# Prologue of a sketched-attention and FFN kernel: key features and kv sums in 32-column tiles, a third of the key products on GpSimd, and another order of the first loads

## The chip, the cores and the metric

The kernel runs on one core of one Trainium2 chip. The metric is the device time of a run in microseconds; a kernel's time is the median of its runs. Engines are named as the profile names them: PE is TensorE's matmul (PEld its weight loads), DVE is VectorE, ACT is ScalarE, POOL is GpSimd, SP is SyncE, which here only issues transfers. A name like "q1" below is a piece of a tensor and is explained where it is used first.

## The reference

The inputs are q, k and v of shape (4 batches, 4 heads, 1088 positions, 32), the two sketches S1 and S2 (8 x 32 each), w_in (128 x 2048) and w_out (2048 x 128), all float32.

```python
def phi(x):                                   # 64 features of a position
    a = einsum('rd,bhsd->bhsr', S1, x)
    b = einsum('rd,bhsd->bhsr', S2, x)
    return einsum('bhsi,bhsj->bhsij', a, b).reshape(..., 64)
q_p, k_p = phi(q), phi(k)
kv = einsum('bhsf,bhsd->bhfd', k_p, v)        # 64 x 32 per head
z = sum(k_p, axis=2)
num = einsum('bhsf,bhfd->bhsd', q_p, kv)
den = einsum('bhsf,bhf->bhs', q_p, z) + 1e-6
x = (num / den) as (4352 tokens, 128)
out = maximum(x @ w_in, 0) ** 2 @ w_out       # (4352, 128)
```

## The kernel before

The attention part is small; the FFN part, 4352 tokens through 128 x 2048 and 2048 x 128, keeps TensorE busy from about 14 us to the end. Tokens are columns of one tile, xT (128 x 4352), and the FFN goes over them in ten chunks (the list FC: 256, 384, 448, 448, 512 ... 256 columns). For every chunk 16 blocks of 128 hidden units are made: `pg` (L582, w_in times xT), a relu on ScalarE (L591), a square on ScalarE or VectorE (L599, L601), and `po` (L620, w_out times the square, summed over the blocks). Chunk 0 is columns 0 to 255 of batch 0, chunk 1 is columns 256 to 639.

Attention of batch 0 is split into three pieces of 256, 384 and 448 columns. The first piece is done by a prologue written out by hand (L678 to L810), so that the FFN can start before the rest. Everything behind it is put in order by a small planner at build time (`_Order`): each task has an engine, an estimated duration and a key, and the planner emits the instructions of all engines in the order of its simulated schedule. The engines then run their own queues strictly in that order; the planner does not see what the chip does.

The prologue, in the order that matters:

- Loads. S1 and S2 are issued by ScalarE (L216, L217), then two of the four first v parts; all else is issued by SyncE: k in two parts (columns 0 to 511 and 512 to 1087), q's first 256 columns (q0), v (four parts for tiles 0 to 3, then four for tiles 4 to 8), q's columns 256 to 639 (q1), w_in in four quarters (wi0 to wi3, 256 KB each), q's columns 640 on (q2), w_out in four quarters (wo0 to wo3, 256 KB each). There are eight landing semaphores used in turn by all loads, so an issue waits in its queue until the load eight places before it has landed.
- `keep_warm` (L668) makes ten matmuls of constants while the loads run.
- k is transposed by VectorE (`a_kT0`, L287) into kt0; S1 and S2, side by side in s_nat, into s_T (L681). Small copies on three engines spread s_T into the block forms sf (L686, for k) and sq (L689 to L696, for q).
- `a_kf` (L310): one matmul per tile of 128 positions, kt0 as weights (128 x 128), sf as the moving side (64 columns); it gives both sketches of k in PSUM (kf). ScalarE copies the second half to kb (L319). A float32 matmul appears in the trace as two passes, so that nine matmuls are 18 records.
- `a_kp0` (L326): VectorE multiplies kf by kb to the 64 features of each head, in four instructions of 2, 2, 3 and 2 tiles.
- `q0(x)` (L719) makes both sketches of q's first 256 columns (x0); ScalarE copies one (qb0), VectorE multiplies (qp0, L741).
- `a_kv0` (L380): per tile and head one matmul with 64 columns of features as weights and 32 columns of v and 32 of ones as the moving side, summed in PSUM (kvp).
- From kvp VectorE makes block-diagonal weights bd (L757), a copy kvt (L766) and zm (L768). TensorE makes den and num of the first piece (L783) and two helper products (L790, L426); VectorE divides (L803 to L808) and writes xT's columns 0 to 255.

GpSimd, besides small copies, casts w_in's quarters into the type that the `pg` matmuls take (`cast_wi`, L663). Its queue then holds the 16 copies `rd` (`a_rl`, L491) that bring the reciprocals of the second piece of batch 0 (columns 256 to 639) into place; they come after the fourth cast, in program order and by an explicit dependence on ("wi", 3). VectorE turns rd into bc (L545) and multiplies it with nd to xT (L552), which chunk 1 of the FFN reads.

## Time and profile before

| What | Value |
|---|---|
| median of 3 runs | 187.94 us (187.44 to 187.97) |
| span of the profiled execution | 185.6 us |
| rest of a run, median less span | 2.3 us |
| first FFN product (L582) starts | 13.73 us |
| FFN chunk 1 (128x384 `pg`) starts | 21.99 us |
| PE busy | 180.1 us, 97% of the span |
| DVE, ACT, POOL busy | 59%, 79%, 19% |
| HBM read and written | 8.78 MB and 2.23 MB |

The profile is of one execution. Times are counted from the start of its span, in us; the profile has no separate total time for that execution, so that the 2.3 us around the span are the median of the runs less this span. In a line of groups or of the time line, "out<-in" are the program's names, then come the shape, a count, and in brackets the idle time of the engine before the group with what ended it. "Landing" of a transfer is the moment at which all its parts are reported as written.

### The profile page before, as it was taken

Reading aid. Unit: us, or ns where it says so; the run is one execution under the profiler, and the core shown is the slowest. Engines: PE = TensorE matmul, PEld = TensorE weight load, DVE = VectorE, ACT = ScalarE, POOL = GpSimd, SP = SyncE. Lnnn points to the kernel's source line nnn. Section 1 sums busy time; section 2 is a strip of 40 time slices with the busy share of each in tenths; the row PEclk is TensorE's granted clock in tenths of the full one; section 3 lists DMA queues with packets and bytes.
Section 4 is the critical chain, followed back from the end, with each engine's and each line's share of the span. In section 5 each row is a group of like instructions: output and inputs, shape, how many; then the busy total and the mean of one; then the engine's idle time right before and its main releaser. Section 6 shows DMA issues by size and latency. Waiting matters only on the chain.

```text
span 185.6 us, 3865 instructions
## 1 busy us (share of the span) xinstructions
PE 180.1 (97%) x1466; PEld 104.9 (57%) x1466; DVE 109.4 (59%) x244; ACT 147.4 (79%) x282; POOL 35.5 (19%) x157
## 2 busy tenths in 40 slices
PE   8898999999999999999999999999999999999992
PEld 2766766666656556554454545554555555555791
DVE  4979889958991699599343982996121113112210
ACT  3509778878978989699797996897999999988960
POOL 2725405327400000770000003820000000000000
PEclk9999999999999999999999999999999999999999
DMA  5799900100039600000882100001203000300111
GB/s 176 188 285 322 203 8 5 28 4 0 4 43 250 159 4 0 4 0 8 189 218 42 16 0 4 0 0 22 38 0 58 0 0 5 56 0 0 28 28 28
DMA packets 24673, 11.25 MB, mean 61 GB/s; under 512 B 18000, under 2 KB 23120, under 8 KB 24656
## 3 DMA queue, kind: packets, MB, share of 16 engines
q1 hardware_dynamic: 24144, 10.82, 24.8%
q10 hardware_dynamic: 512, 0.20, 0.4%
q8 instruction: 11, 0.18, 0.4%
q14 instruction: 6, 0.05, 0.1%
HBM read 8.78 MB, written 2.23 MB: 59 GB/s over the span
## 4 chain that ended last, share of the span: by engine, by line
PE 95%; DMA 1%; DVE 1%; ACT 0%; issue 0%; POOL 0%; ACTq 0%; DVEq 0%
PE po L620 60%; PE pg L582 18%; PE nd L535 3%; PE kvp L401 2%; PE pol L615 2%; PE po L615 2%; PE qc L303 2%; DMA s_nat<-in_S_dram 1%; PE kvp L383 1%; PE kf L313 1%; PE kc L303 1%; PE x L722 1%; ACT gt L591 0%; PE warm L671 0%; PE num L783 0%; PE den L783 0%
## 5 line engine op out<-in xcount | busy, mean ns | idle before, releaser
L620 PE MATMUL po<-g,w_o 128*128 128x512 f32 (+3 forms) x288 | 133.2, 546 | 0.0
L582 PE MATMUL pg<-xT,w_in 128*128 128x512 f32 (+3 forms) x160 | 104.5, 663 | 0.5 <-ACT gt L591 0.5
L591 ACT ACTIVATE gt<-pg 128x512 f32<-128x512 f32 (+3 forms) x145 | 80.9, 562 | 21.2 <-PE pg L582 20.5
L599 ACT ACTIVATE g<-gt 128x512 f32<-128x512 f32 (+2 forms) x123 | 72.0, 602 | 2.6
L620 PEld LDWEIGHTS po<-g,w_o 128*128 128x128 f32 x288 | 53.0, 189 | 29.8 <-issue 19.9
L582 PEld LDWEIGHTS pg<-xT,w_in 128*128 128x128 f32 x160 | 30.0, 189 | 31.7 <-issue 15.0
L601 DVE TENSOR_TENSOR g<-gt 128x512 f32<-128x512 f32 (+2 forms) x22 | 14.2, 651 | 41.8 <-ACT gt L591 41.8
L442 POOL COPY kv<-kvt 32x64 f32<-32x64 f32 x48 | 11.6, 241 | 64.7 <-DVE kvt L419 62.6
L496 POOL COPY rd<-rc 32x9 f32<-32x9 f32 (+2 forms) x80 | 16.6, 207 | 12.5 <-DVE rc L488 9.3
L505 DVE STREAM_SHUFFLE qa<-qc 128x576 f32<-128x576 f32 (+2 forms) x20 | 11.6, 647 | 0.0
L520 DVE TENSOR_TENSOR qp<-qa,qb 128x576 f32<-128x576 f32 (+2 forms) x20 | 10.8, 599 | 0.0
L624 DVE STREAM_TRANSPOSE oT<-po 128x512 f32<-128x512 f32 (+3 forms) x9 | 5.9, 652 | 8.1 <-PE po L620 8.1
L468 DVE STREAM_TRANSPOSE qt<-qc 128x576 f32<-128x576 f32 (+2 forms) x10 | 5.8, 614 | 6.0 <-PE qc L303 6.0
L354 DVE TENSOR_TENSOR kp<-fs 128x576 f32<-128x576 f32 x12 | 8.2, 741 | 0.0
L535 PE MATMUL nd<-qp,kv 32*32 32x288 f32 (+2 forms) x320 | 6.8, 353 | 0.0
L552 DVE TENSOR_TENSOR xT<-nd,bc 128x576 fp32r<-128x576 f32 (+2 forms) x10 | 5.6, 600 | 1.1 <-PE nd L535 1.1
L545 DVE STREAM_TRANSPOSE bc<-rd 128x576 f32<-128x576 f32 (+2 forms) x10 | 5.8, 598 | 0.7 <-POOL rd L496 0.6
L345 DVE STREAM_TRANSPOSE fs<-kc 128x576 f32<-128x576 f32 x6 | 4.3, 762 | 3.1 <-PE kc L303 3.1
L535 PEld LDWEIGHTS nd<-qp,kv 32*32 32x32 f32 x320 | 3.8, 103 | 4.0 <-issue 2.2
L505 DVE STREAM_SHUFFLE qb<-qc 128x576 f32<-128x576 f32 (+2 forms) x10 | 6.0, 648 | 0.0
L296 DVE STREAM_TRANSPOSE qT<-qn 128x192 f32<-128x192 f32 (+3 forms) x11 | 5.8, 562 | 0.0
L615 PE MATMUL pol<-w_o,g 128*128 128x128 f32 x32 | 5.7, 275 | 0.0
(94 smaller groups left out, 94.2 us busy)
## 6 DMA issues: line engine op xcount, KB each, us to landing
kn<-in_k_dram SPq DMA_DIRECT2D x3, 544.0 KB, 5.3
qn<-in_q_dram SPq DMA_DIRECT2D x3, 544.0 KB, 6.6
vn<-in_v_dram SPq DMA_DIRECT2D x9, 144.0 KB, 5.2
w_in<-in_moe_w_in_dram SPq DMA_DIRECT2D x4, 256.0 KB, 5.0
w_o<-in_moe_w_out_dram SPq DMA_DIRECT2D x4, 256.0 KB, 7.7
out_dram<-oT SPq DMA_DIRECT2D x12, 64.0 KB, 2.0
out_dram<-oT SPq DMA_DIRECT2D x8, 56.0 KB, 1.9
out_dram<-oT SPq DMA_DIRECT2D x8, 48.0 KB, 1.8
```

Of the source, the lines that this page charges most:

```text
L354: nc.vector.tensor_tensor(out=_ap(st[b, "kp"], 0, 128, 2 * o, [[64, NT], [8, 8], [1, 8]]), in0=_ap(fs, 0, 128, o, [[32, NT], [1, 8], [0, 8]]),
L442: nc.gpsimd.tensor_copy(_ap(st[b, "kv"], 32 * c, 32, 64 * h, [[32, E], [1, 32]]), _ap(st["kvt"], 32 * h, 32, 0, [[64, E], [1, 32]]),)
L496: nc.gpsimd.tensor_copy(st[b, "rd", i0][32 * h : 32 * h + 32, n * c : n * c + n], st["rc"][32 * c : 32 * c + 32, n * h : n * h + n],)
L505: nc.vector.stream_shuffle(in_=banks(st[b, "qc", i0], 2 * x, 0, m), out=_ap(st[b, which, i0], 0, 128, 2 * m * x, [[m, 2], [1, m]]), mask=m ...
L520: nc.vector.tensor_tensor(out=st[b, "qp", i0, e][:, r], in0=st[b, f"qa{e}", i0][:, r], in1=st[b, "qb", i0][:, r], op=mult,)
L535: nc.tensor.matmul(nd[32 * h : 32 * h + 32, 512 * c : 512 * c + m], kv[r, o : o + 32], qp[r, m * h : m * h + m], start=(e == 0), stop=(e = ...
L582: nc.tensor.matmul(st["pg", u][:, n * i : n * i + n], w_in[:, 128 * (d0 + i) : 128 * (d0 + i) + 128], xT[:, c0 : c0 + n],)
L591: nc.scalar.activation(gt[:, 0:w], st["pg", u][:, 0:w], Relu)
L599: nc.scalar.activation(g2[:, 0:w], gt[:, 0:w], Square)
L601: nc.vector.tensor_tensor(out=g2[:, 0:w], in0=gt[:, 0:w], in1=gt[:, 0:w], op=mult)
L615: nc.tensor.matmul(po[x // 128][:, 0:128], g[:, x : x + 128], w, start=(d == 0), stop=(d == NB - 1),)
L620: nc.tensor.matmul(po[0][:, 0:n], w, g, start=(d == 0), stop=(d == NB - 1))
```

## The change

- S2 is issued first on ScalarE's queue; S1 goes second on SyncE's, behind the first part of k. The second part of k and q0 go to ScalarE's queue, all eight v parts to SyncE's.
- The weights and the rest of q come in the order wi0, q1, wo0, wi1, wo1, wi2, wo2, q2, wi3, wo3 (before: q1, wi0, wi1, q2, wo0, wi2, wi3, wo1, wo2, wo3).
- Nine constant matmuls in place of ten.
- On GpSimd the four irep copies and two memsets come before the copies that wait for s_T, and the two sw copies behind them; it takes over one sf copy and two sq copies. VectorE's sf copies go to ScalarE (two) and GpSimd.
- VectorE transposes s_T before k, and k in the order tiles 0 to 3, 7 to 8, 4 to 6.
- `a_kf` makes four matmuls of 32 columns per tile in place of one of 128; `a_kv0` makes two of 32 in place of one of 64.
- Tiles are grouped as 2, 2, 2 and 3. The product of the last three (128x768) is made by GpSimd; for it ScalarE copies both halves of kf (192 columns, kab) out of PSUM.
- On VectorE, qT of columns 256 to 447 and s2f stand ahead of bd, the other qT (448 to 639) behind it; kvt is copied by ScalarE.
- The instruction in L776, a GpSimd copy that only made its queue wait for kp, is gone.

The planner and all behind the prologue are unchanged, and so is the order of instructions there on each engine.

```diff
-    W0, W3, W4 = 10, 1, 1
+    POOL_T = 6
+    W0, W3, W4 = 9, 1, 1
...
-    nc.scalar.dma_start(s_nat[0:8, :], S1[:, :])
+    load_k(nc.sync, 0, 0, 512)
     nc.scalar.dma_start(s_nat[8:16, :], S2[:, :])
-    load_k(nc.sync, 0, 0, 512)
-    load_k(nc.sync, 0, 512, S)
-    load_q(nc.sync, 0, 0, 256)
+    nc.sync.dma_start(s_nat[0:8, :], S1[:, :])
+    load_k(nc.scalar, 0, 512, S)
+    load_q(nc.scalar, 0, 0, 256)
...
-    load_v(nc.sync, 0, 0, 0, 4)
-    load_v(nc.scalar, 0, 2, 0, 4)
-    load_v(nc.sync, 0, 1, 0, 4)
-    load_v(nc.scalar, 0, 3, 0, 4)
+    for p in range(4):
+        load_v(nc.sync, 0, p, 0, 4)
     for p in range(4):
         load_v(nc.sync, 0, p, 4, NT)
+    load_wi(nc.sync, 0)
     load_q(nc.sync, 0, 256, 640)
-    load_wi(nc.sync, 0)
+    load_wo(nc.sync, 0)
     load_wi(nc.sync, 1)
+    load_wo(nc.sync, 1)
+    load_wi(nc.sync, 2)
+    load_wo(nc.sync, 2)
     load_q(nc.sync, 0, 640, S)
-    load_wo(nc.sync, 0)
-    load_wi(nc.sync, 2)
     load_wi(nc.sync, 3)
-    load_wo(nc.sync, 1)
-    load_wo(nc.sync, 2)
     load_wo(nc.sync, 3)
...
-    def a_kf(t0, n, pool, tag):
+    def a_kf(t0, n, pool, tag, pool_too=False):
         kf = pool.tile([128, 512], F32, tag=tag, name="kf")
         for t in range(n):
-            nc.tensor.matmul(
-                _ap(kf, 0, 128, 32 * t, [[32 * n, 2], [1, 32]]),
-                kt0[:, 128 * (t0 + t) : 128 * (t0 + t) + 128],
-                sf[:, 0:64],
-            )
-        kb = wpool.tile([128, 32 * 3], F32, tag="kb", bufs=4, name="kb")
-        nc.scalar.copy(kb[:, 0 : 32 * n], kf[:, 32 * n : 64 * n])
+            for c in range(4):
+                o = 128 * (t0 + t) + 32 * c
+                nc.tensor.matmul(
+                    _ap(kf, 32 * c, 32, 32 * t, [[32 * n, 2], [1, 32]]),
+                    kt0[:, o : o + 32],
+                    sf[:, 0:64],
+                )
+        if pool_too:
+            kb = wpool.tile([128, 64 * 3], F32, tag="kab", bufs=1, name="kab")
+            nc.scalar.copy(kb[:, 0 : 64 * n], kf[:, 0 : 64 * n])
+        else:
+            kb = wpool.tile([128, 32 * 2], F32, tag="kb", bufs=3, name="kb")
+            nc.scalar.copy(kb[:, 0 : 32 * n], kf[:, 32 * n : 64 * n])
...
-        nc.vector.tensor_tensor(
+        own = t0 == POOL_T
+        (nc.gpsimd if own else nc.vector).tensor_tensor(
...
     def a_kv0(t):
         for h in range(H):
-            i, y, o, o_v = h % 2, h // 2, 64 * (H * t + h), 32 * (NT * h + t)
-            nc.tensor.matmul(
-                st[0, "kvp"][64 * i : 64 * i + 64, 64 * y : 64 * y + 64],
-                st[0, "kp"][:, o : o + 64],
...
+            i, y, o_v = h % 2, h // 2, 32 * (NT * h + t)
+            for x in range(2):
+                r, o = 64 * i + 32 * x, 64 * (H * t + h) + 32 * x
+                nc.tensor.matmul(
+                    st[0, "kvp"][r : r + 32, 64 * y : 64 * y + 64],
+                    st[0, "kp"][:, o : o + 32],
...
-    a_kf(2, 2, psf, "pg")
-    a_kf(4, 3, psf, "po")
-    a_kf(7, 2, psf, "pg")
+    a_kf(2, 2, psf, "po")
+    a_kf(6, 3, psf, "pg", True)
+    a_kf(4, 2, psf, "pg")
...
-    for t0, n in ((0, 2), (2, 2), (4, 3), (7, 2)):
+    for t0, n in ((0, 2), (2, 2), (4, 2), (6, 3)):
...
-    nc.vector.transpose(s2f[:, :], _ap(sf, 0, 128, 72, [[0, 4], [1, 8]]))
...
-    for i0 in (8, 14):
-        a_qT(0, i0, 6)
+    a_qT(0, 8, 6)
+    nc.vector.transpose(s2f[:, :], _ap(sf, 0, 128, 72, [[0, 4], [1, 8]]))
...
-    nc.vector.tensor_copy(st["kvt"][:, :], st[0, "kvp"][:, 0:128])
+    nc.scalar.copy(st["kvt"][:, :], st[0, "kvp"][:, 0:128])
...
     a_bd(0)
+    a_qT(0, 14, 6)
...
-    nc.gpsimd.tensor_copy(zero_a[:, 0:1], st[0, "kp"][:, 256 * NT - 1 : 256 * NT])
```

More of the change, by code (lines that the diff above doesn't have):

```diff
@@ L261 @@
     make_identity(nc, iden[:])
+    for h in range(H):
+        nc.gpsimd.tensor_copy(
+            _ap(irep, 32 * h, 32, 0, [[32, 4], [1, 32]]),
+            _ap(iden, 32 * h, 32, 32 * h, [[0, 4], [1, 32]]),
+        )
+    nc.gpsimd.memset(_ap(vn[1], 96, 32, 32 * (NT - 2), [[32 * NT, H], [1, 64]]), 0.0)
+    nc.gpsimd.memset(_ap(pd, 0, 128, 8, [[9, 4 * NT], [1, 1]]), 1e-6)
     own_f, s2f, zm = sb("own_f", 16), sb("s2f", 32), sb("zm", 32)
@@ L307, in sketch @@
                 )
-    def a_kf(t0, n, pool, tag):
+    def a_kf(t0, n, pool, tag, pool_too=False):
         kf = pool.tile([128, 512], F32, tag=tag, name="kf")
         for t in range(n):
-            nc.tensor.matmul(
-                _ap(kf, 0, 128, 32 * t, [[32 * n, 2], [1, 32]]),
-                kt0[:, 128 * (t0 + t) : 128 * (t0 + t) + 128],
-                sf[:, 0:64],
-            )
-        kb = wpool.tile([128, 32 * 3], F32, tag="kb", bufs=4, name="kb")
-        nc.scalar.copy(kb[:, 0 : 32 * n], kf[:, 32 * n : 64 * n])
+            for c in range(4):
[4 more added lines that the diff above has]
+                    sf[:, 0:64],
+                )
+        if pool_too:
[4 more added lines that the diff above has]
+            nc.scalar.copy(kb[:, 0 : 32 * n], kf[:, 32 * n : 64 * n])
         st["kf", t0] = kf, kb
@@ L328, in a_kp0 @@
         kf, kb = st["kf", t0]
-        nc.vector.tensor_tensor(
+        own = t0 == POOL_T
+        (nc.gpsimd if own else nc.vector).tensor_tensor(
             out=_ap(st[0, "kp"], 0, 128, 256 * t0, [[64, 4 * n], [8, 8], [1, 8]]),
-            in0=_ap(kf, 0, 128, 0, [[8, 4 * n], [1, 8], [0, 8]]),
-            in1=_ap(kb, 0, 128, 0, [[8, 4 * n], [0, 8], [1, 8]]),
+            in0=_ap(kb if own else kf, 0, 128, 0, [[8, 4 * n], [1, 8], [0, 8]]),
+            in1=_ap(kb, 0, 128, 32 * n if own else 0, [[8, 4 * n], [0, 8], [1, 8]]),
             op=mult,
@@ L381, in a_kv0 @@
         for h in range(H):
-            i, y, o, o_v = h % 2, h // 2, 64 * (H * t + h), 32 * (NT * h + t)
-            nc.tensor.matmul(
-                st[0, "kvp"][64 * i : 64 * i + 64, 64 * y : 64 * y + 64],
-                st[0, "kp"][:, o : o + 64],
-                _ap(vn[0], 0, 128, o_v, [[VC - o_v, 2], [1, 32]]),
-                start=(t == 0 and y == 0),
-                stop=(t == NT - 1),
-                skip_group_check=True,
-            )
+            i, y, o_v = h % 2, h // 2, 32 * (NT * h + t)
[4 more added lines that the diff above has]
+                    st[0, "kp"][:, o : o + 32],
+                    _ap(vn[0], 0, 128, o_v, [[VC - o_v, 2], [1, 32]]),
+                    start=(t == 0 and y == 0),
+                    stop=(t == NT - 1),
+                    skip_group_check=True,
+                )
     def a_kv(b, t, x, start=False):
@@ L679 @@
     keep_warm(W0)
+    nc.vector.transpose(s_T[:, :], s_nat[:, :])
     a_kT0(0, 4)
-    nc.vector.transpose(s_T[:, :], s_nat[:, :])
+    a_kT0(7, 2)
+    a_kT0(4, 3)
     for h, eng in (
-        (0, nc.gpsimd.tensor_copy), (1, nc.vector.tensor_copy), (2, nc.scalar.copy),
-        (3, nc.vector.tensor_copy),
+        (0, nc.gpsimd.tensor_copy), (1, nc.scalar.copy), (2, nc.gpsimd.tensor_copy),
+        (3, nc.scalar.copy),
     ):
@@ L694 @@
     )
-    for h, eng in ((1, nc.scalar.copy), (2, nc.gpsimd.tensor_copy), (3, nc.scalar.copy)):
-        eng(
+    for h in range(1, H):
+        nc.gpsimd.tensor_copy(
             _ap(sq, 32 * h, 32, 64 * (h % 2), [[128, 2], [1, 64]]),
@@ L701 @@
         nc.gpsimd.tensor_copy(sf[32 * h : 32 * h + 32, 64:96], s_T[:, :])
-    for h in range(H):
-        nc.gpsimd.tensor_copy(
-            _ap(irep, 32 * h, 32, 0, [[32, 4], [1, 32]]),
-            _ap(iden, 32 * h, 32, 32 * h, [[0, 4], [1, 32]]),
-        )
-    nc.gpsimd.memset(_ap(vn[1], 96, 32, 32 * (NT - 2), [[32 * NT, H], [1, 64]]), 0.0)
-    for w in sw:
-        nc.gpsimd.tensor_copy(w[:, :], sf[:, 64:96])
-    nc.gpsimd.memset(_ap(pd, 0, 128, 8, [[9, 4 * NT], [1, 1]]), 1e-6)
-    a_kT0(4, 3)
-    a_kT0(7, 2)
     a_qT(0, 0, 8)
@@ L733 @@
     nc.scalar.copy(_ap(qb0, 0, 128, 0, [[256, 2], [1, 256]]), banks(x0, 0, 0, 256))
-    st[0, "kvp"] = psf.tile([128, 512], F32, tag="pg", name="kvp")
-    for t0, n in ((0, 2), (2, 2), (4, 3), (7, 2)):
+    st[0, "kvp"] = psf.tile([128, 512], F32, tag="po", name="kvp")
+    for t0, n in ((0, 2), (2, 2), (4, 2), (6, 3)):
         a_kp0(t0, n)
@@ L738 @@
             a_kv0(t)
-    nc.vector.transpose(s2f[:, :], _ap(sf, 0, 128, 72, [[0, 4], [1, 8]]))
+    for w in sw:
+        nc.gpsimd.tensor_copy(w[:, :], sf[:, 64:96])
     nc.vector.tensor_tensor(
```

## The prediction

> **What bounds the kernel now.** I read the page's first part, then the chain that ended last in order of time, then the time line from 13 to 22 us, then the transfers one by one, with times to landing.

> ```profile
> PE 180.1 (97%) x1466; PEld 104.9 (57%) x1466; DVE 109.4 (59%) x244; ACT 147.4 (79%) x282; POOL 35.5 (19%) x157
> ...
> PEclk9999999999999999999999999999999999999999
> ```

> TensorE is busy for 97% of the span at full clock. Only the start, where PE waits or does small work, can give anything back.

> ```profile
> 1.54 2.73 DMA s_nat<-in_S_dram
> ...
> 5.18 2.19 PE kf L313 x18
> 7.37 1.06 PE x L722 x8
> 8.44 2.25 PE kvp L383 x72
> 10.69 0.58 PE den L747 x4
> ```

> The chain (start, duration) begins with the landing of S1 and S2 at 4.27. Then come k features, x0, the kv sums, and at 14.06 the first FFN product. All this the change wants shorter. But the kernel has a second path to the same place:

> ```profile
> 16.22 0.62 POOL L664 CAST w_in<-w_in 128x512 fp32r<-128x512 f32 x1 [1.59 <-DMA w_in<-in_moe_w_in_dram]
> 16.78 4.15 POOL L496 COPY rd<-rc 32x3 f32<-32x3 f32 x16
> ```

> ```profile
> 20.96 0.38 DVE L545 STREAM_TRANSPOSE bc<-rd 128x192 f32<-128x192 f32 x1 [0.58 <-POOL rd L496]
> ...
> 21.26 0.58 DVE L552 TENSOR_TENSOR xT<-nd,bc 128x192 fp32r<-128x192 f32 x2
> ...
> 21.96 0.19 PEld L582 LDWEIGHTS pg<-xT,w_in 128*128 128x128 f32 x1 [0.17 <-ACT g L599]
> 21.99 0.41 PE L582 MATMUL pg<-xT,w_in 128*128 128x384 f32 x1
> ```

> GpSimd waits 1.59 us for the last quarter of w_in, casts it, and only then makes the 16 copies rd (0.26 us each); VectorE waits for them, makes bc and xT; PE starts FFN chunk 1 (columns 256 to 639) at 21.99. xT is complete at 21.84, and PE's product before it started at 21.59 and runs about 0.4: both paths meet within 0.1 us. rc, which the copies read, was ready at 15.98, so the copies are tied to the landing of w_in's quarter 3. **So chunk 1 cannot start earlier than that landing plus 5.8 us**, whatever is won before it, and behind it PE is saturated.

> **The change, part by part.**

> *S1 and S2 on two queues.* Now S1 is issued at 0.92 and S2 at 1.54 on ScalarE's queue. S1 landed at about 3.4 (SyncE's issue that waits for it starts at 3.40), S2 at 4.27. After: S2 takes S1's place, S1 follows the first k part (issued 0.74, landed 3.50) on SyncE's queue, so about 3.5. s_T moves before the k transpose: it ends near 3.8 instead of 4.58, 0.8 earlier. GpSimd must first finish what was moved ahead: irep 4 x 0.34, two memsets 0.31 and 0.16, from 2.10 to 3.95; its two sf copies end near 4.4. The 0.71 transpose of k's first part ends near 4.45. So kf starts near 4.55 instead of 5.18: -0.6.

> *k features in 32 columns.* 9 matmuls of two passes become 36 of two: 72 passes of 128 rows x 32 columns with 64 moving columns. The trace has this very shape:

> ```profile
> 38.26 1.21 PE L401 MATMUL kvp<-kp,vn 128*32 128x64 f32 x72
> ```

> so kf costs about 1.2 instead of 2.19, -1.0. Below: 1.03 (the start of the next line's passes, 39.29 less 38.26). Above: no gain, 2.19. I take 1.2, the same shape, in which a pass starts every 1.03 / 72 = 14 ns. [...] But the later kf parts wait for k's second part (now issued 1.19, landed 4.19): it goes on ScalarE's queue behind S2, from 1.54, beside v on the other queue: landing near 4.6, then transposes 0.33 + 0.54, so kf ends near 6.3 (7.37 before). x0 (1.06) needs q's first part (landed 5.57; same size, I leave it there) and ends near 7.3: -1.1.

> *kv sums.* 36 matmuls become 72, 144 passes; 144 x 14 ns = 2.05 against 2.25 for 72 passes of 64 columns: -0.2. VectorE makes three products of 0.58 (start to start) and ends near 7.7 instead of 8.86. GpSimd's 128x768 product has no row. Below 0.9: cast rows, 0.616 for 512 elements. Above 2.2: two reads and a write each at the slope of GpSimd's rows, (0.616-0.189)/496 = 0.86 ns. I take 1.7, between them, since it reads two inputs where the cast reads one. It starts near 6.8 (its three sq copies at 0.34 and four sf copies at 0.24 come first), so ends near 8.5; PE wants it after 6 of 9 tiles, near 8.6. kvp ends near 9.5 instead of 10.69: -1.1. If the product costs 2.2, -0.7.

> *What waits behind kvp.* VectorE's queue now has qT of columns 256 on (0.37) and s2f (0.19) ahead of bd. That qT waits for q's second part, landed at 9.14 when it was first after v; now it is second, behind 256 KB of w_in (in before the next 256 KB landed 1.24 after it). SyncE issues w_in's quarter 0 near 5.7 and q near 6.2. So q lands between 9.1 and 10.3, I take 9.9; bd starts near 10.5 instead of 10.73, not at 9.6. Queued behind it: bd, zm, dT, and with them PE's den. kvt on ScalarE adds two hand-overs (bd, kvt, zm), some 0.3 on the last bd, hidden by PE's den pair and x (1.2 from first bd to num). First FFN product: -0.2, between -1.1 and +0.2.

> *Loads of the weights.* Order before: q1, wi0, wi1, q2, wo0, wi2, **wi3**, wo1, wo2, wo3. After: wi0, q1, wo0, wi1, wo1, wi2, wo2, q2, **wi3**, wo3. wi3 goes from seventh to ninth: 512 KB more ahead of it. Transfers, each asked for by its own window (last number: us to landing):

> ```profile
> w_in<-in_moe_w_in_dram SPq DMA_DIRECT2D x1, 256.0 KB, 7.3
> ```
> ```profile
> w_o<-in_moe_w_out_dram SPq DMA_DIRECT2D x1, 256.0 KB, 7.7
> ```

> These are wi3, issued 8.86, landed 16.17; and wo2, issued 9.81, landed 17.53. The bytes that were in by wo2 are those that must now be in by wi3. Both orders are long enough that the queue never runs dry. The stream could start sooner; how much it can gain the windows show (DMA share, GB/s at the end):

> ```profile
> 6.00:7.00 1.00, 1.00 (x12) 1.00 (x11) 1.00 (x3) 0.31 (x3) 0.80 (x5) 1.00 0.48 118
> 7.00:8.00 1.00, 1.00 (x10) 0.89 (x11) 1.00 (x2) 0.41 (x2) 0.88 (x4) 1.00 0.72 204
> 8.00:9.00 1.00, 1.00 (x26) 0.67 (x24) 0.98 (x3) 0.52 (x1) 0.66 (x5) 1.00 0.95 214
> 9.00:10.00 1.00, 1.00 (x42) 1.00 (x40) 0.90 (x3) 0.07 (x1) 0.12 (x1) 1.00 0.63 171
> ```

> Unfilled in these four: 1.2 us. Weights start about 0.2 earlier (the last v part no longer waits for q's landing at 5.57). I take 0.4 earlier in all: wi3 lands at 17.1 (bounds 17.5 and 16.0). [...]

> **The sum.** wi3 0.93 later: cast to 17.8, rd copies to 21.9, xT near 22.8, chunk 1 near 22.9 instead of 21.99. PE itself would be there at 21.8. What the prologue won is waited away, and +0.9 remains. Other weights arrive in time: wi1 near 12.2 for a use near 14.8, wi2 near 14.3 for one near 16.5, wo1 and wo2 earlier than now. Span 185.6 becomes 186.5; the median of the runs, 187.94, lies 2.3 above the span, which I leave unchanged: **188.8**.

> **Rivals.**
> 1. *The stream speeds up, and the change is faster.* The same 2.26 MB (q1 to wo2) took from 7.0 to 17.0, 226 GB/s; 11 to 17 us ran at 268 to 400. w_in alone, 8 to 10 us, was slow (214, 171); mixed with w_o it may not be. From an average of 257 GB/s, wi3 lands at 16.1 and the loss is gone; at 310 it lands near 14.8 and PE decides, with the -0.2 to -1.1 above. Price: -0.8, 187.1. Against: the slow stretch may belong to a first touch of w_in, which stays.
> 2. *A tie.* The lull closes wholly (1.2): wi3 at 16.3, +0.1, 188.0. This is also the case that the change's parts work but are hidden.
> 3. *Two losses.* GpSimd's product costs over 3 us, or PE's wait of 1 us and more before chunk 1 lowers the clock. For the first: kvp, casts and FFN start all slip past before's times; for the second, the present waits of up to 0.66 left the clock at 1.00, which does not show a longer one. Price: some 1.5 more, 190.3.

> **Chances.** Forecast 0.57 (188.2 to 189.5), faster stream 0.22, tie 0.10, two losses 0.11. Some 0.1 of the forecast lies under 188.5, so faster by over 0.3% (about what a measurement of this kernel can tell from no change) 0.21, within it 0.20, slower 0.59. The range, 187.2 to 190.0, leaves out half of the faster case and half of the two losses.

> **What would show it.** Right: POOL's fourth cast waits for w_in until about 17.1; rd copies start near 17.8; PE idles over 0.5 us before the first 128x384 pg; kf's passes take 14 to 17 ns each and kvp ends near 9.5; bd waits behind qT for q. Wrong: the fourth cast starts before 16.2, or PE meets no wait at chunk 1; the GpSimd product over 2.2; kf's passes over 25 ns.

## The result and the profile after

The kernel after takes 190.63 us (median of four runs; 188.97 to 192.38) against 187.94: 1.0126 times as long, interval 1.0095 to 1.0158. The prediction was 188.8, with a range up to 190.0: the sign was right, the loss is about three times as large (2.7 us by the medians, 2.4 by the ratio, against 0.9). Every ratio here is made on one chip and leaves out runs over 1.5% above the kernel's own fastest; of E2's four runs that leaves one (191.06 us), and the profiles of E2 (194.38 us) and E12 (190.57 us) are of runs left out.

The profiled execution took 191.28 us, its span 189.4, against 185.6 before. First the page, the line of TensorE's busy time and the granted clock in 40 slices:

```profile
PE 182.4 (96%) x1590; PEld 105.0 (55%) x1591; DVE 108.1 (57%) x240; ACT 147.3 (78%) x282; POOL 37.8 (20%) x160
...
PEclk9975999999999999999999999999999999999999
```

PE is busy 2.3 us longer, and the clock, a row of nines before, shows 7 and 5 in the third and fourth slice (9.5 to 19 us). PE's time line there (start, duration, operation, count, idle time before it):

```profile
4.78 1.54 PE L318 MATMUL kf<-sf,kt 128*32 128x64 f32 x72
6.25 1.13 PE L725 MATMUL x<-qT,sq 64*128 64x256 f32 x8
7.32 2.09 PE L395 MATMUL kvp<-vn,kp 128*32 128x64 f32 x131
11.53 0.64 PE L395 MATMUL kvp<-vn,kp 128*32 128x64 f32 x13 [2.12 <-issue]
12.10 1.12 PE L751 MATMUL den<-eps 1*64 1x256 f32 x4
...
17.36 1.26 PE L594 MATMUL pg<-xT,w_in 128*128 128x256 f32 x4
...
25.80 0.52 PE L594 MATMUL pg<-xT,w_in 128*128 128x384 f32 x1
```

In the kernel before, the same line of products runs without a wait:

```profile
8.37 2.32 PE L383 MATMUL kvp<-vn,kp 128*64 128x64 f32 x72
10.62 0.65 PE L747 MATMUL den<-eps 1*64 1x256 f32 x4
...
13.73 0.80 PE L582 MATMUL pg<-xT,w_in 128*128 128x256 f32 x4
```

Up to 9.4 us all goes as predicted: the kv sums start 1.05 us earlier than before (7.32, 8.37) and a pass starts every 14.4 ns. Then, with 131 of 144 passes done, PE stands still for 2.12 us. "issue" means that it waited for nothing that the profile shows. What follows takes longer than before: `den<-eps` 1.12 where it took 0.65. The same stretch by windows (start:end, length, busy time and count of PE, PEld, DVE, ACT, POOL, then the granted clock, DMA share, GB/s):

```profile
9.00:10.00 1.00, 0.41 (x27) 0.26 (x16) 0.00 (x0) 0.00 (x0) 0.14 (x1) 1.00 0.89 280
10.00:11.00 1.00, 0.00 (x0) 0.00 (x0) 0.00 (x0) 0.00 (x0) 0.48 (x1) 1.00 0.65 207
11.00:12.00 1.00, 0.47 (x13) 0.40 (x12) 0.28 (x1) 0.00 (x0) 0.00 (x0) 0.74 0.86 258
12.00:14.00 2.00, 2.00 (x13) 0.59 (x8) 1.15 (x6) 0.27 (x1) 0.62 (x1) 0.50 1.03 346
```

From 10 to 11 us no computing engine but GpSimd, which casts w_in, does anything. The clock record then says 0.5 from 11.48 to 18.31 us.

The whole difference, from three points of the two time lines: `den<-eps` starts at 12.10 instead of 10.62 (+1.48: 1.05 won, then 2.12 of standstill and thirteen slow passes); from there to the first FFN product 5.26 us instead of 3.11 (+2.15: half clock); from there to chunk 1 8.44 instead of 8.26 (+0.18). Together 3.8, the difference of the spans. Chunk 1 itself starts with no wait of PE.

VectorE shows a second wait at the same place:

```profile
8.05 0.69 DVE L745 TENSOR_TENSOR qp<-x,qb 128x512 f32<-128x512 f32 x1 [0.45 <-ACT qb L736]
11.72 0.38 DVE L299 STREAM_TRANSPOSE qT<-qn 128x192 f32<-128x192 f32 x1 [2.97 <-DMA qn<-in_q_dram]
12.02 0.17 DVE L756 STREAM_TRANSPOSE s2f<-sf 128x32 f32<-128x32 f32 x1
12.22 0.29 DVE L761 TENSOR_TENSOR bd<-kvp,own_p 128x128 f32<-128x128 f32 x1
```

q1 landed at 11.69. It came in sixteen slices; fifteen of these were in by 10.19, the last came 1.5 us later. Which transfer ran just then? The queues of the window 9.0 to 9.6 us (packets, MB, share of the 16 engines):

```profile
q1 hardware_dynamic: 309, 0.18, 97.0%
q8 instruction: 1, 0.02, 9.7%
```

One packet of q8, "instruction": 16 KB, started at 9.31, 0.93 us long. Before, the first such packet of the span comes at 13.73. The page counts 12 of them instead of 11. No view names the engine that such a packet is for; that these are PE's is inferred, from the counts that follow.

### The profile page after: what moved, and what is told of

It reads as the page before. It is cut to its first block, busy times and chain, and to the rows that moved or that the text cites. A ratio compares the mean times of both kernels' runs of the same rounds, so it can differ in the third digit from the quotient of the medians.

```text
span 189.4 us, 4110 instructions
## 1 busy us (share of the span) xinstructions
PE 182.4 (96%) x1590; PEld 105.0 (55%) x1591; DVE 108.1 (57%) x240; ACT 147.3 (78%) x282; POOL 37.8 (20%) x160
## 4 chain that ended last, share of the span: by engine, by line
PE 94%; DMA 2%; issue 1%; DVE 1%; ACT 0%; ACTq 0%
PE po L632 59%; PE pg L594 18%; PE nd L547 3%; PE kvp L413 2%; PE pol L627 2%; PE po L627 2%; DMA kn<-in_k_dram 2%; PE qc L306 2%; PE kvp L395 1%; PE kc L306 1%; PE x L725 1%; PE den L787 1%; PE num L787 1%; PE den L751 1%; DVE kt L293 0%
## 5 line engine op out<-in xcount | busy, mean ns | idle before, releaser
L613 DVE TENSOR_TENSOR g<-gt 128x512 f32<-128x512 f32 (+2 forms) x22 | 14.3, 652 | 42.0 <-ACT gt L603 41.8
## 6 DMA issues: line engine op xcount, KB each, us to landing
w_in<-in_moe_w_in_dram SPq DMA_DIRECT2D x4, 256.0 KB, 5.7
w_o<-in_moe_w_out_dram SPq DMA_DIRECT2D x4, 256.0 KB, 5.6
```

Source lines behind the costliest of these rows:

```text
L613: nc.vector.tensor_tensor(out=g2[:, 0:w], in0=gt[:, 0:w], in1=gt[:, 0:w], op=mult)
```

## The theories

- **Theory 1**: PE runs out of instructions. The 32-column tiles need 126 passes more ahead of the FFN (k features 72 instead of 18, kv sums 144 instead of 72), and the next 16 KB block comes behind the loads.
- **Theory 2**, the one on record: late loads, q1 for bd and wi3 for chunk 1.
- **Theory 3**: the clock goes down by itself, because the new prologue gives PE less work.

A fourth came up on the way: k's second part, moved to ScalarE's queue.

## The experiments

All results in one table; the columns behind the ratio are of one profiled execution each, in us.

| Kernel | ratio to before (95%) | first FFN product | chunk 1 | longest idle PE from k features on | half clock |
|---|---|---|---|---|---|
| before | 1 | 13.73 | 21.99 | 0.51, sq | none |
| after | 1.0126 (1.0095 to 1.0158) | 17.36 | 25.80 | 2.12, issue | 11.48 to 18.31 |
| E1 after, kv sums 64 | 1.0151 (1.0108 to 1.0195) | 16.83 | 25.43 | 2.01, bd | 12.41 to 19.23 |
| E2 after, k features 128 | none (191.06 us) | 18.90 | 28.91 | 2.60, issue | 7.90 to 11.31, 18.14 to 24.97 |
| E3 after, loads as before | 1.0062 (1.0025 to 1.0098) | 15.03 | 24.11 | 1.35, kt | none |
| E4 after, 90 matmuls more | 1.0158 (1.0097 to 1.0220) | 17.40 | 25.52 | 1.24, issue | no record before 11.53 |
| E5 after, kv sums 64, qT behind bd | 1.0070 (1.0038 to 1.0101) | 14.05 | 23.09 | 0.85, kt | none |
| E6 after, qT behind bd | 1.0088 (1.0057 to 1.0120) | 14.79 | 22.81 | 1.58, issue | none |
| E7 before, k features 32 | 1.0022 (0.9999 to 1.0044) | 13.04 | 21.15 | 0.48, relu | none |
| E8 before, loads as after | 1.0018 (1.0001 to 1.0034) | 13.86 | 22.33 | 0.48, relu | none |
| E9 before, k features 64 | 0.9997 (0.9976 to 1.0019) | 13.16 | 21.42 | 0.49, relu | none |
| E10 E5, k features 64, loads as before | 1.0019 (0.9985 to 1.0053) | 14.06 | 23.61 | 1.13, kt | none |
| E11 E10, k, q0, v on the queues as before | 0.9994 (0.9975 to 1.0013) | 13.37 | 21.39 | 0.50, kt | none |
| E12 E7 again | 1.0035 (1.0013 to 1.0057) | 13.10 | 21.22 | 1.40, issue | 25.59 to 29.01 |

**E1. Kv sums in 64 columns again.**

```diff
-            for x in range(2):
-                r, o = 64 * i + 32 * x, 64 * (H * t + h) + 32 * x
...
+                st[0, "kvp"][64 * i : 64 * i + 64, 64 * y : 64 * y + 64],
+                st[0, "kp"][:, o : o + 64],
```

> After, with the kv sums back in 64 columns (36 matmuls, 72 passes, instead of 72 and 144); all else stays. Theory 1 (PE ran out of instructions: it stood still from 9.41 to 11.53 us after 450 PE records, while a 16 KB block of instructions started at 9.31 behind the weight loads; the standstill then cost the full clock for 6.83 us): with 144 records fewer the same count falls behind the first FFN products, no idle time of the kind 'issue' near 9.4 us, clock 1.0 throughout, the first FFN product near 13.5 us instead of 17.4, about 187 to 188 us. Theory 2 (the one on record: late loads, q's second part holding bd and the fourth quarter of w_in holding chunk 1): the time stays within 0.3 of the recorded 188.8 us, and 0.2 above what the kernel after would have without the standstill. Theory 3 (the clock goes down by itself because the changed prologue gives PE less work in a window): the half clock stays, 190 to 191 us.

No gain (the interval overlaps that of after): theory 1, as it stood, was wrong on the time. The standstill of the kind "issue" is gone, but at the same place stands another of the same length:

```profile
9.95 0.65 PE L749 MATMUL den<-eps 1*64 1x256 f32 x4
12.61 1.12 PE L785 MATMUL den<-qp,bd 128*64 128x256 f32 x4 [2.01 <-DVE bd L759]
```

bd waits behind qT for q1, which landed at 11.89, its last slice 1.44 behind the fifteenth; the instruction packet ran at 9.51. PE idles for 2 us, and the clock falls for 6.83 us all the same. So the kernel after has two waits, one behind the other.

**E2. K features in 128 columns again.**

```diff
-            for c in range(4):
...
+                kt0[:, 128 * (t0 + t) : 128 * (t0 + t) + 128],
```

> After, with the k features back in 128 columns (9 matmuls, 18 passes, instead of 36 and 72); all else stays. Theory 1: the 450th PE record, behind 108 fewer, now lies behind the kv sums; the standstill of 2.1 us inside kvp and the half clock go, though this edit is nowhere near kvp in the code; k features cost 1.0 us more, so 187.5 to 188.5 us, 2 to 3 below the kernel after. Theory 2: 1.0 us is lost that the late loads cover, so no change against after. Theory 3: the standstill stays where it was, 190 to 191 us.

The standstill left the kv sums, as theory 1 says, but did not vanish:

```profile
9.86 2.89 PE L393 MATMUL kvp<-vn,kp 128*32 128x64 f32 x144
...
15.35 0.37 PE L306 MATMUL qc<-qT,sw 32*32 32x96 f32 x11
18.33 0.59 PE L306 MATMUL qc<-qT,sw 32*32 32x96 f32 x21 [2.60 <-issue]
```

It stands in the middle of another product (qc), 5 us later. Count PE's passes ahead of it: 9 + 18 + 8 + 144 + 4 + 4 + 8 + 8 + 4 + 1 + 11 = 219. In the kernel after: 9 + 72 + 8 + 131 = 220. It is the count that is the same, not the place.

**E3. Order of the weight loads as before.**

```diff
-    load_wi(nc.sync, 0)
     load_q(nc.sync, 0, 256, 640)
-    load_wo(nc.sync, 0)
+    load_wi(nc.sync, 0)
     load_wi(nc.sync, 1)
...
```

> After, with the order of the loads behind v as in the kernel before (q's second part first, then w_in 0 and 1, q's third part, w_o 0, w_in 2 and 3, w_o 1 to 3). Theory 2: this gives back what the late loads took: the fourth cast starts near 16 us, chunk 1 near 22, about 188 us or less, 2.5 below after. Theory 1: the block of instructions still comes behind the loads, the standstill in kvp of 1.5 to 2.5 us and the half clock stay, and the time stays within 0.7 us of the kernel after (189.5 to 191).

The standstill stays, again after pass 220, but is shorter, because PE was held up earlier by k's second part:

```profile
6.94 0.77 PE L318 MATMUL kf<-sf,kt 128*32 128x64 f32 x40 [1.35 <-DVE kt L293]
...
8.70 2.09 PE L395 MATMUL kvp<-vn,kp 128*32 128x64 f32 x131
11.48 0.42 PE L395 MATMUL kvp<-vn,kp 128*32 128x64 f32 x13 [0.69 <-issue]
```

The clock holds, and the time is 1.2 us (0.6% of 188) below after, though the two intervals still touch. Neither theory's number is met: 0.69 of standstill is under theory 1's 1.5 to 2.5, 189.2 above theory 2's 188. Chunk 1 waits 0.71 us for xT here: wi3 landed at 18.27.

**E4. More instructions ahead.**

```diff
-    keep_warm(W0)
+    for i in range(96):
+        nc.tensor.matmul(
+            st["warm"][32 * (i % 4) : 32 * (i % 4) + 32, 0:64],
...
+    keep_warm(3)
```

> After, with 96 small matmuls (32 columns of weights, 64 moving columns, bf16, on constants) in place of six of the nine that keep PE warm at the start: some 180 more PE records ahead of the k features, and no other change. The work that matters is the same, and instructions are added. Theory 1: the limit of a block is crossed near the start, so the next block is asked for before the weight loads begin; no standstill in kvp, clock 1.0 from before the k features to the end, first FFN product near 13.5 us, 187 to 188 us. If the small matmuls lower the clock at the start, kf and x start some 0.5 us later. Theory 2: no change, 188.8 by the record, or like the kernel after. Theory 3 (less dense work of PE): the half clock stays or gets longer, 190 to 192 us.

As a test of the time it failed: the small matmuls took only 1.47 us, PE idled 1.16 us before the k features, and these, x and kvp ran slower (x in 2.08 us instead of 1.13); the clock's record of 1.0 begins at 11.53. But the standstill moved as theory 1 says. The kv sums run through, and it comes here:

```profile
14.40 0.43 PE L793 MATMUL num<-qp,bd 128*64 128x256 f32 x1
16.08 0.65 PE L793 MATMUL num<-qp,bd 128*64 128x256 f32 x3 [1.24 <-issue]
```

That is after pass 348 = 220 + 128. If the 128 passes between are one 16 KB packet, that makes 128 bytes a pass, an estimate from the packet's size and these two counts. The number of packets, if all are PE's, agrees with it: 11 for the 1466 passes of before, 12 for the 1590 of after, 13 for the 1681 of E4, which makes 129 to 133 passes a packet.

**E5 and E6. VectorE's transpose of q1 behind bd**, with the kv sums in 64 columns (E5) and in 32 (E6).

```diff
-    a_qT(0, 8, 6)
     nc.vector.transpose(s2f[:, :], _ap(sf, 0, 128, 72, [[0, 4], [1, 8]]))
...
     a_bd(0)
+    a_qT(0, 8, 6)
     a_qT(0, 14, 6)
```

> After with two edits: the kv sums back in 64 columns, and VectorE's transpose of q's columns 256 to 447 moved behind bd, zm and bd. Theory 1, as the first runs have changed it (PE asks for its next block of instructions early in the prologue; the block, one 16 KB packet of 0.93 us near 9.4 us, does harm twice: PE waits for it where the instructions run out, and the slice of q's second part behind it lands 1.4 us after the other fifteen, so that bd waits): with both waits taken away bd starts near 10.1 us, PE has no idle time over 0.7 us before the first FFN product, which starts near 13.5 us, the clock is 1.0 from about 5.6 us on, and the time is 187 to 188.8 us, 2 to 3 below kv sums alone (190.6). Theory 2 (the record: w_in's fourth quarter at 17.1 us holds chunk 1): chunk 1 near 23 us with PE waiting 0.5 to 1 us for xT, 188.8 us; this can hold beside theory 1. Theory 3 (the clock goes down without an idle PE): half clock again, 190 us or more.

> After with one edit: VectorE's transpose of q's columns 256 to 447 moved behind bd, zm and bd; the kv sums stay in 32 columns. Theory 1: bd still has to wait for the last kv sums, which wait for PE's instructions until about 11.5 us, so the standstill of PE near 9.4 us and the half clock stay, 190 to 191 us: each of the two waits hides the other, and one alone gains under 0.5 us. Theory 2 (q's landing alone holds PE): bd near 10 us, no half clock, 188 to 188.8 us.

With E1 these are the four corners of two edits: neither 1.0126, kv sums alone 1.0151, qT alone 1.0088, both 1.0070. The intervals part E5 from E1 (by 1.5 us, where 2 to 3 were expected); E6 overlaps both after and E5. In E6 the standstill is there after pass 220 (1.58 us), in E5 there is none, and bd starts at 10.40:

```profile
11.04 0.42 PE L395 MATMUL kvp<-vn,kp 128*32 128x64 f32 x13 [1.58 <-issue]
```

```profile
8.04 2.32 PE L393 MATMUL kvp<-vn,kp 128*64 128x64 f32 x72
10.29 0.65 PE L749 MATMUL den<-eps 1*64 1x256 f32 x4
10.87 0.65 PE L785 MATMUL den<-qp,bd 128*64 128x256 f32 x4
...
14.05 0.71 PE L592 MATMUL pg<-xT,w_in 128*128 128x256 f32 x4 [0.32 <-POOL w_in L674]
```

E6 did better than expected: in its profile the clock held through 1.58 us of idle PE. But that is the fastest of its ten runs (187.95 us); in two others the mean clock is 0.991, and in the three of 190.78 to 192.53 us it is 0.972 to 0.982. Theory 3 falls with the profiles of E3, E5 and E6: the new prologue, and no half clock. And with both waits gone, the step on record appears in E5, first on GpSimd, then on PE:

```profile
17.41 0.61 POOL L674 CAST w_in<-w_in 128x512 fp32r<-128x512 f32 x1 [2.06 <-DMA w_in<-in_moe_w_in_dram]
17.97 4.06 POOL L506 COPY rd<-rc 32x3 f32<-32x3 f32 x16
```

```profile
21.86 0.59 PE L630 MATMUL po<-g,w_o 128*128 128x256 f32 x2
23.09 0.41 PE L592 MATMUL pg<-xT,w_in 128*128 128x384 f32 x1 [0.64 <-DVE xT L562]
```

**E7, E12 and E9. Before, with the k features alone in 32 columns (twice; the edit of `a_kf` shown above with the change), and in 64 (the edit here).**

```diff
-            nc.tensor.matmul(
-                _ap(kf, 0, 128, 32 * t, [[32 * n, 2], [1, 32]]),
...
+            for c in range(2):
+                o = 128 * (t0 + t) + 64 * c
+                nc.tensor.matmul(
+                    _ap(kf, 64 * c, 64, 32 * t, [[32 * n, 2], [1, 32]]),
+                    kt0[:, o : o + 64],
...
```

> Before, with one edit: the k features in 32-column tiles (36 matmuls of 72 passes instead of 9 of 18). Theory 1: 108 more PE records ahead of the kv sums, so that the block of instructions is asked for 1.5 us and more earlier and its packet comes near 10 to 11.5 us instead of 13.73; by then q's second part is in (9.14 before), and the instructions last until the first FFN products, so no standstill over 0.5 us; the k features take 1.2 us instead of 2.19, and the time is 0 to 0.8 us below before, held by w_in's fourth quarter and the copies rd. Theory 2: chunk 1 stays at 22 us because of w_in's fourth quarter, so the same as before within 0.3 us. Theory 3: less work of PE per us in the prologue, clock down, 189 us or more.

> The same kernel as the k features in 32 columns alone, run again for a second profile: its first set had one run at 186.4 us, the profiled one, and nine at 187.5 to 188.3. If the packet of instructions at 8.8 us hits another load from run to run, this profile shows a late slice of w_in or q (over 1 us behind the other fifteen) and a later chunk 1, near 22 us; if the profile is again like the first, the cause of the spread stays open.

> Before, with one edit: the k features in tiles of 64 columns (18 matmuls, 36 passes). A kv pass on a 64-column tile takes 2.25 / 72 = 31 ns, so the k features should take about 1.1 us, like the 1.2 of 32 columns, with 36 passes fewer. Theory 1: the packet of PE's instructions comes later than with 32 columns (8.76 us) and finds fewer loads that somebody waits for; no standstill; 0.2 to 1 us below before, and steadier than the k features in 32 columns alone. Theory 2: chunk 1 is held by w_in's fourth quarter and the copies rd, so within 0.3 us of before.

In the first profile of the k features in 32 columns everything is as wished: 1.30 us instead of 2.19, chunk 1 at 21.15, span 184.6; only the packet came earlier than expected, at 8.76. That run took 186.41 us; the other nine of its set took 187.5 to 188.3, no faster than before. The second profile, of a run of 190.57 us, shows one way in which more is lost:

```profile
22.71 0.71 PE L303 MATMUL kc<-kT,sf 32*32 32x288 f32 x14
24.82 0.73 PE L303 MATMUL kc<-kT,sf 32*32 32x288 f32 x18 [1.40 <-issue]
25.48 2.00 PE L622 MATMUL po<-g,w_o 128*128 128x256 f32 x4
```

After pass 342 (six short of 348) PE waits 1.40 us, by theory 1 for the next block (a packet starts at 22.21), and the clock is half for 3.41 us; what late slices would show (the expectation's guess) isn't seen. The nine slower runs of the first set aren't explained by it: their mean clock is 0.997 to 1.0, and what holds them stays open. In 64 columns the k features take 1.32 us, the same, with half the passes; no standstill, and the time is that of before.

**E8. Before, with the order of the loads of after.**

> Before, with one edit: the order of the loads behind v as in the kernel after (w_in 0 ahead of q's second part, w_in 3 ninth instead of seventh). Theory 2, the step on record: w_in's fourth quarter lands near 17.1 us instead of 16.17, the copies rd start near 17.8, PE waits before chunk 1, which starts near 22.9 instead of 21.99: 0.9 us above before. Theory 1: the instructions are those of before, so the packet stays near 13.7 us and nothing waits for it; q's second part lands near 10 and holds bd by at most 0.3 us: 0 to 0.3 us above before, and w_in's fourth quarter, whose slice no longer lies behind the packet, lands no later than 16.5.

```profile
16.50 0.61 POOL L664 CAST w_in<-w_in 128x512 fp32r<-128x512 f32 x1 [2.33 <-DMA w_in<-in_moe_w_in_dram]
...
22.33 0.41 PE L582 MATMUL pg<-xT,w_in 128*128 128x384 f32 x1
```

wi3 lands at 16.45, not 17.1, and chunk 1 starts at 22.33, 0.34 us later than before; the ratio also comes to 0.34 us, with an interval from 0.02 to 0.64. Theory 1's bounds nearly hold (0.3; the packet at 13.09, q1 at 9.99). The order of the loads alone costs, by these, a little over a third of the 0.9 that I charged.

**E10 and E11. What can be saved of the change.** Part of the edit from E10 to E11 is shown; v's first parts go back to both queues too.

```diff
     load_k(nc.sync, 0, 0, 512)
...
-    load_k(nc.scalar, 0, 512, S)
-    load_q(nc.scalar, 0, 0, 256)
+    load_k(nc.sync, 0, 512, S)
+    load_q(nc.sync, 0, 0, 256)
...
```

> After with four edits: k features and kv sums in tiles of 64 columns, VectorE's transpose of q's columns 256 to 447 behind bd, and the order of the weight loads as before. PE's instructions then last until the FFN, and bd waits for no load. What is left of the change is S1 and S2 on two queues, k's second part and q's first part on ScalarE's queue, v on SyncE's alone, the product on GpSimd. Theory 1: no standstill, clock 1.0, first FFN product near 13.2 us, 186.8 to 187.8 us. Theory 4 (found in the first runs: k's second part, now on ScalarE's queue, lands at 4.6 to 6.0 us where it landed at 4.19, with its last slice up to 1.4 us behind the others; PE waits for it between the k features, and SyncE's later loads are issued behind it): PE idle 0.5 to 1.4 us between the k features, w_in's fourth quarter at 17 us or later, 188 to 189 us.

> As the kernel with four edits, and k's second part and q's first part back on SyncE's queue, v's first parts on both queues as before; S1 and S2 stay on two queues. Theory 4: k's second part lands near 4.3 us, no idle PE over 0.3 us between the k features, SyncE issues its loads earlier, w_in's fourth quarter lands before 16.5 us, 186.3 to 187.3 us, the fastest so far. Theory 1 alone: the same as the kernel with four edits within 0.3 us.

In E10 k's second part lands at 5.70 (its fifteenth slice at 5.26), and PE waits:

```profile
6.62 0.80 PE L318 MATMUL kf<-sf,kt 128*64 128x64 f32 x20 [1.13 <-DVE kt L293]
```

SyncE's next issue that uses k's landing semaphore waits too (5.72), and with it all behind it: w_in's first quarter is issued at 7.51. In E11 k lands at 5.01, that issue comes at 5.03 and w_in's at 6.33; PE waits 0.50, w_in's fourth quarter lands at 14.89 instead of 17.60, and chunk 1 starts at 21.39, 0.6 us earlier than in the kernel before. So theory 4 is right in direction, with smaller numbers than expected (k at 5.01, not 4.3). That the queue is the cause is not shown: q0 and v's parts moved with k, and in the profile of after k landed at 4.64 from ScalarE's queue, earlier than here from SyncE's. The two intervals of the ratios overlap; the profiles differ, the times are not told apart. Neither beats the kernel before. In E9 and E11 the median span is 0.55 to 0.7 us shorter than before on the same chip (185.1 and 185.25 against 185.8), but the time outside the span is longer, 2.03 and 2.16 us against 1.79. Why it is, stays open.

## Why the prediction was wrong

**The arithmetic of the prologue was right in the main.** K features end at 6.3 (predicted 6.3), x0 at 7.4 (7.3), the first 131 kv passes at the rate of a 9.6 end (9.5), the GpSimd product from 6.95 to 8.46 in 1.51 us (6.8 to 8.5 in 1.7). One small term was not there: a kv pass on a 32-column tile starts every 14.4 ns, as predicted, but on a 64-column tile every 29.5, not 31, so that the 0.2 put down for the finer kv sums is about 0.05. The 25 ns a pass named as a sign against the forecast comes from no run; in E7 a pass of the k features started every 17 ns ((6.55 - 5.32) / 72).

**Step 1 that failed: the kv sums, "144 x 14 ns = 2.05", "kvp ends near 9.5".** It prices a pass by its duration alone. In place of the end at 9.5 came 2.12 us of standstill. By theory 1 a pass also has instructions that must be brought in, by a packet among the loads (in after, 9.0 to 9.6 us, q1 97.0% and q8 9.7%), and small tiles use them up faster: at 14.4 ns 128 passes of kvp last 1.8 us. That is inferred from the counts. Six profiles show the standstill, and the table shows what they have in common (packets from the trace's transfer records):

| Kernel | passes before it | packet starts, lasts | PE goes on | behind the packet's end |
|---|---|---|---|---|
| after | 220 | 9.31, 0.93 | 11.53 | 1.29 |
| E2 | 219 | 16.04, 0.88 | 18.33 | 1.41 |
| E3 | 220 | 8.69, 1.55 | 11.48 | 1.24 |
| E6 | 220 | 8.61, 1.07 | 11.04 | 1.36 |
| E4 | 348 | 13.78, 0.93 | 16.08 | 1.37 |
| E12 | 342 | 22.21, 1.14 | 24.82 | 1.47 |

The count is the same, or larger by 122 or 128 passes (the profile does not count register, branch and semaphore instructions, so that it need not be exact), and PE resumes 1.24 to 1.47 us after the packet. The kernel before, which reaches pass 220 at 19.5 us, shows no such standstill (longest idle 0.51). What decides when a packet starts, the trace does not show; in E2 it was 16.04 and in E6 8.61. But in all fourteen profiles the first one starts after PE's 89th pass, 0.3 us (E3: 8.39, 8.69) to 4.8 us later (E2: 11.25, 16.04). So it may be asked for about there, 131 passes ahead of the standstill, and then wait behind the loads; that is inferred.

**Step 2 that failed: "q lands between 9.1 and 10.3, I take 9.9; bd starts near 10.5".** q1 landed at 11.69. I had seen that qT was put in front of bd, and what that would cost if q1 were late, but not what makes it late. With a packet of instructions just before or during q1 its last slice is 0.78 to 1.81 us behind the fifteenth (after 1.50, E1 1.44, E3 1.81, E5 0.78, E6 1.03); without one it is 0.02 to 0.40 (E2, E4, E7 to E12), and 0.72 in the kernel before. That the slice lies behind the packet on one of the 16 DMA engines is inferred: the trace does not name a packet's engine, and a late slice alone does not show a packet, for the last of k's second part came 0.65 to 1.03 us late in E2, E3 and E4 with no packet in the span before it.

**Step 3: rival 3's "lowers the clock".** I gave the rival a tenth, with the wait before chunk 1 as the place. (The 0.66 that I gave as the longest present wait was that of a weight load; the matmuls waited 0.51 at most once they had begun.) What it feared came in another place: 2.12 us of idle PE, and 2.15 us lost at half clock until the first FFN product. The runs of the kernel after show it too: mean clock 0.997, 0.991 and 0.981 go with spans of 187.1, 188.1 and 189.4. One stretch of 3.41 us at half clock, as in E12, is 3.41 x 0.5 / 188 = 0.009 of the mean clock, so by this estimate these fit none, one and two such stretches, at 1.0 to 1.3 us each; two make the 6.83 us of the profile.

**The step on record, "wi3 0.93 later", was real but too large, and stood in the second row.** In the profile of after wi3 landed at 16.44, 0.27 later than before, and decided nothing, for the copies waited for rc, which was late by the rest; that the forecast had the right sign is luck here (GpSimd's time line of after):

```profile
16.49 0.62 POOL L676 CAST w_in<-w_in 128x512 fp32r<-128x512 f32 x1 [1.39 <-DMA w_in<-in_moe_w_in_dram]
19.86 4.26 POOL L508 COPY rd<-rc 32x3 f32<-32x3 f32 x16 [2.75 <-DVE rc L500]
```

In E5, with the two waits gone, the cast waits until 17.41 (predicted 17.1), the copies start at 17.97 (17.8), chunk 1 at 23.09 with PE waiting 0.64 (22.9, over 0.5). E5's time is 0.70% above before, 1.3 us; the sum on record was 0.9. But the reason was wrong in part: the order of the loads alone brings 0.34 (E8). The rest goes with a stream that starts late: w_in's first quarter was issued at 5.73 in E8 and at 6.69 in E5, where SyncE's issues wait 1.7 us for k, and wi3 landed at 16.45 and 17.35. The slow first touch of w_in, named against rival 1, is shown by no run; from 8 to 10 us the kernel after moved 256 and 280 GB/s, the kernel before 214 and 171.

## What to carry over

Count instructions, not only their time: where small tiles are cut finer, multiply the passes and compare with the count at which PE stood still (here 220, and 342 or 348); the same speed was to be had for the k features with half the passes (64 columns: 1.32 us for 36, 32 columns: 1.30 for 72). When one wait is taken away and nothing moves, look for a second wait of the same length in its place before dropping the theory. And a queue that waits for a load early in the kernel holds up the loads behind it: SyncE issued w_in's first quarter at 7.51 in E10, where k landed at 5.70, and at 6.33 in E11, where it landed at 5.01.
